# Moving a norm and a matrix difference in two slabs of a fused attention and MoE kernel, and storing the last slab with one DMA per 128-row block

## The chip, the cores and the metric

The kernel runs on one core of a Trainium2 chip. The metric is device time in microseconds (us); a profiled execution is taken apart instruction by instruction. The engines are TensorE (PE in the profile, its weight loads PEld), VectorE (DVE), ScalarE (ACT), GpSimd (POOL) and SyncE (SP), which here only issues DMAs and waits. Sixteen DMA engines move the data.

## The reference, cut to what matters

Attention with a softmax of its own on q and on k, eight batches of eight heads, 576 positions, head size 64; then a gated layer over all 4608 tokens of width 512 with 2048 hidden units:

```python
q_s = exp(q - max(q, -1));  q_s = q_s / (sum(q_s, -1) + 1e-9)     # over the head size
k_s = exp(k - max(k, 2));   k_s = k_s / (sum(k_s, 2) + 1e-9)      # over the positions
kv  = einsum('bhsd,bhse->bhde', k_s, v)
x   = einsum('bhsd,bhde->bhse', q_s, kv)   # -> (4608, 512), heads side by side
h   = x @ w_in;  g = h * sigmoid(beta * h);  out = g @ w_out
```

The kernel leaves the maxima out (the inputs are small) and works in bfloat16 between the stages.

## The kernel before, in words

**Slabs.** The tokens are cut into nine slabs of 512. Slab t below 8 holds the first 512 positions of batch t; slab 8 holds the last 64 positions of all eight batches. For every slab `pass1_tile` and `pass1_lead` multiply x by `w_in` (line 406) and ScalarE applies the gate into `GT` (L744), VectorE scaling it (L767). Then `pass2_fast` multiplies by `w_out` (L844). It uses a scheme with seven block products in place of eight: sums of gate halves (`g_sum1`, `g_sum2`), differences of gate halves (`g_diff`, L810, one VectorE instruction of 128x2048 elements each, in place in `GT`) and sums and differences of the weights.

**Pass 2 in order.** TensorE runs the products into three PSUM banks s, z5 and z2: s and the first part of z5, then z2 with `gs2(1)`, z5 with `gt(0, 0)`, z2 with `gt(NG, 1)`, z5 with `gt(0, 1)`, and z2 with `gt(NG, 0)`. The two products named last read what `g_diff(0)` and `g_diff(1)` have made: z5's last one the first, z2's last one the second. ScalarE empties z5 and z2 once each in between (`copy`, L880), and VectorE adds at the end (`last`, L892). z2's last product also needs ScalarE's copy out of z2, since it writes that bank again. `hooks` holds callbacks that are run at numbered places between those steps (`at(0)` to `at(7)`).

**Attention for the next batch** is woven into the slabs. `exp_q`, `exp_k` and `exp_kr` are ScalarE exponentials. `norm_main(b, hp0, n, eng, sums, mult)` normalises n head pairs of q: a VectorE sum (L357), a reciprocal (L359), and the multiply (L361), on VectorE or GpSimd. `turn` transposes the result with a DMA on SP's queue (L606), `norm_turn` is both with the multiply on GpSimd. Casts of v run on GpSimd (`casts`). `kv_steps` are the key-value products on TensorE (L482), after which VectorE writes a reciprocal and `KVD` (L490, L459). `quad(b, (g,))` (L554) multiplies the transposed q by `KVD`, half a batch at a time in slabs 1 to 3; the first half needs the first transpose DMA, the second half the second one. These steps are put in at counts of TensorE work: `todo` holds pairs of a count and a step, and `tick` runs the ones that are due. For slabs 1 and 2 `attn_late` puts the key-value products at 100 or 97 and the first half of `quad` at 118; the second half comes at 1.5 in the next slab.

**Order on each engine** is the order of recording: `add` appends an instruction to its engine's list, and `Program.plan` derives the semaphore waits from what is read and written. [...] A DMA's issue is one instruction of SP's or ScalarE's list, its end a semaphore of its own.

**Slabs 1 and 2 at place 3** run `diffs_norm`, one VectorE sequence:

```python
norm_main(b, 2, 2, mult=False)   # sum, reciprocal
g_diff(0); g_diff(1)
norm_main(b, 2, 2, sums=False)   # multiply, on VectorE
turn(b, 2, 2)
```

**The end.** Slabs 0 to 7 are stored by one DMA each on SP. Slab 8 is stored by `store8` as its parts get ready: `O2S[0]` holds four blocks of 128 rows, each made of 64 rows of two batches (the two partition halves), in two column halves. `emit` ends SP's list with a wait for each output semaphore, in the order of their names.

Of the kernel before, what the change touches and what calls it, by code (L numbers as in the profile page):

```python
# [7 lines left out]
ACT = mybir.ActivationFunctionType  # L8
# [5 lines left out]
S = 576  # L14
D = 64
NTOK = B * S
DM = H * D
# [6 lines left out]
SM = 512  # L24
# [5 lines left out]
PE, ACTE, DVE, POOL, SP = "tensor", "scalar", "vector", "gpsimd", "sync"  # L30
# [14 lines left out]
class Program:  # L45
# [12 lines left out]
    def add(self, eng, fn, r=(), w=(), bank=(), slot=None, after=(), war=False):  # L58
        op = Op(eng, fn, slot)
        op.pos = len(self.ops)  # L60
        deps = op.deps
        deps.extend(after)
        for k in r:
            deps.extend(self.writer.get(k, ()))
            self.readers.setdefault(k, []).append(op)
        for k in w:
            for d in self.readers.get(k, ()):
                if d is not op and (war or not self._same(d, op)):
                    deps.append(d)
            for d in self.writer.get(k, ()):  # L70
                if not self._same(d, op):
                    deps.append(d)
            self.readers[k] = []
            self.writer[k] = [op]
        for k in bank:
            t = self.touch.setdefault(k, {})
            for e, d in t.items():
                if e != eng:
                    deps.append(d)
            t[eng] = op  # L80
        if eng == POOL and slot is None:
            if self.pool is not None:
                deps.append(self.pool)
            self.pool = op
        self.ops.append(op)
        return op
# [42 lines left out]
    def emit(self, nc, es):  # L129
        counts, waits = self.plan()  # L130
        sems = {}
        for key in counts:
            sems[key] = es.enter_context(nc.semaphore("s_" + "_".join(str(x) for x in key)))
        by = {e: [] for e in (PE, ACTE, DVE, POOL, SP)}
        for op, w in zip(self.ops, waits):
            by[op.eng].append((op, w))

        def run(eng):
            def body(h):
                for op, w in by[eng]:  # L140
                    for key, n in w:
                        h.wait_ge(sems[key], n)
                    ins = op.fn(h)
                    if op.slot is not None:
                        ins.then_inc(sems[op.count[0]], 16)
                    elif op.inc:
                        ins.then_inc(sems[op.count[0]], 1)
                if eng == SP:
                    for key, n in sorted(counts.items(), key=str):
                        if key[0] == "dma" and str(key[1]).startswith("out"):  # L150
                            h.wait_ge(sems[key], n)
            return body

        with nc.Block() as blk:
            for e in (PE, ACTE, DVE, POOL, SP):
                getattr(blk, e)(run(e))


def bass_efficient_attn_shen__then__act_swish_beta_kernel(
# [10 lines left out]
    win_h, wout_h, beta_h, out_h = moe_w_in.tensor, moe_w_out.tensor, moe_beta.tensor, out.tensor  # L170

    with ExitStack() as es:
# [53 lines left out]
        add = P.add  # L226
# [122 lines left out]
        def norm_main(b, hp0, n, eng=DVE, sums=True, mult=True):  # L349
            i = b % 2  # L350
            a = bass.AP(EQ[i], hp0 * 512, [[2048, 128], [64, 8 * n], [1, 64]])
            s_ = bass.AP(QS[i], hp0 * 8, [[32, 128], [1, 8 * n]])
            v_ = bass.AP(QI[i], hp0 * 8, [[32, 128], [1, 8 * n]])
            vb = bass.AP(QI[i], hp0 * 8, [[32, 128], [1, 8 * n], [0, 64]])
            ks = [("eq", i, hp) for hp in range(hp0, hp0 + n)]
            if sums:
                add(DVE, lambda e: e.tensor_reduce(s_, a, AX.X, ALU.add), r=ks,  # L357
                    w=[("qs", i, hp0)])
                add(DVE, lambda e: e.reciprocal(v_, s_), r=[("qs", i, hp0)], w=[("qi", i, hp0)])  # L359
            if mult:  # L360
                add(eng, lambda e: e.tensor_tensor(a, a, vb, ALU.mult), r=ks + [("qi", i, hp0)],  # L361
                    w=ks)
# [239 lines left out]
        def turn(b, hp0, n):  # L602
            i = b % 2
            o = bass.AP(QT[i], hp0 * 512, [[2048, 128], [128, 4 * n], [1, 128]])
            a = bass.AP(EQ[i], hp0 * 512, [[2048, 128], [1, 512 * n]])
            add(SP, lambda e: e.dma_start_transpose(o, a),  # L606
                r=[("eq", i, hp) for hp in range(hp0, hp0 + n)],
                w=[("qt", i, hp) for hp in range(hp0, hp0 + n)], slot=f"tq{i}{hp0}")
# [14 lines left out]
        def one(fn, *a):  # L623
            return lambda: fn(*a)

        def steps(fn, *a):
            return lambda: go(fn(*a))
# [7 lines left out]

        def attn_late(b):
            if b < 4:
                return [(100 if b == 2 else 97, steps(kv_all, b)), (118, one(quad, b, (0,)))]
            return [(96, steps(kv_all, b)), (99, lambda: g_diff(1)), (112, one(quad, b))]

        def spread(steps, lo, hi):
# [135 lines left out]
            add(SP, lambda e: e.dma_start(a, O2S[t % 2][:, :, :]),  # L777
                r=[("o2", t % 2, u, d) for u in range(4) for d in range(2)], slot=f"out{t % 2}")

        def store8(th, dh, u=None):  # L780
            us = (0, 1) if u is None else (u,)
            n = len(us)
            for h in range(2):
                a = bass.AP(out_h, ((4 * th + h + 2 * us[0]) * S + SM) * DM + 256 * dh,
                            [[DM, 64], [2 * S * DM, n], [1, 256]])
                o = O2S[0][64 * h:64 * h + 64, 2 * th + us[0]:2 * th + us[0] + n,
                           256 * dh:256 * dh + 256]
                add(SP if h == 0 else ACTE, lambda e, o=o, a=a: e.dma_start(a, o),
                    r=[("o2", 0, 2 * th + u_, dh) for u_ in us], slot=f"outr{th}{dh}{h}{us[0]}")

        def gv(f, th, n):
            return GT[:, f:f + n, 256 * th:256 * th + 256]
# [15 lines left out]
        def g_diff(fh):  # L808
            f, th = NG * fh, 1 - fh
            add(DVE, lambda e: e.tensor_tensor(gv(f, th, NG), gv(f, th, NG), gv(f, 1 - th, NG),  # L810
                                               ALU.subtract),
                r=gk(f, 0, NG) + gk(f, 1, NG), w=gk(f, th, NG), war=True)
# [20 lines left out]
        def pass2_fast(t, tick, hooks):  # L833
# [53 lines left out]
            def last(bk, th, dh):  # L887
                o, w = out(th, dh)
                ts = TS[:, :].rearrange("p (a b) -> p a b", b=256)
                h = halves(bk)  # L890
                for b_, u0, u1 in h:
                    add(DVE, lambda e, b_=b_, u0=u0, u1=u1: e.tensor_tensor(  # L892
                        o[:, u0:u1, :], ts[:, u0:u1, :], bank3(b_)[:, u0:u1, :], ALU.add),
                        r=["ts", ("ps", b_)], w=w[u0:u1], bank=[b_])
                    if t == 8 and len(h) == 2:
                        store8(th, dh, u0)
                if t == 8 and len(h) == 1:
                    store8(th, dh)

# [53 lines left out]
        for t in range(NSLAB):  # L953
# [88 lines left out]
            def on(n, fn, *a):  # L1042
                hooks.setdefault(n, []).append(lambda: fn(*a))
# [4 lines left out]
                if b % 2 == 0:  # L1048
                    exp_kr(b)

            def diffs_norm(b):
                norm_main(b, 2, 2, mult=False)
                g_diff(0)
                g_diff(1)
                norm_main(b, 2, 2, sums=False)
                turn(b, 2, 2)

            def casts(b):
                g = P.writer[("gs2", NG - 1)]
# [5 lines left out]
            if t == 1:  # L1065
                on(0, exps, 2)
                on(0, casts, 2)
                on(2, norm_turn, 2, 0)
                on(3, diffs_norm, 2)
                on(3, load, 4)  # L1070
            elif t == 2:
                on(0, exps, 3)
                on(2, norm_turn, 3, 0)
                on(3, diffs_norm, 3)
                on(3, load, 5)
                on(4, exp_q, 4)
                on(4, casts, 4)
                on(6, norm_turn, 4, 0)
            elif t == 3:
                on(0, exp_k, 4)  # L1080
                on(0, exp_kr, 4)
                on(0, exp_q, 5)
                on(3, g_diff, 0)
                on(4, norm_turn, 5, 0)
                on(5, norm_turn, 5, 2)
                on(4, exp_qr, 1)
                on(5, exp_k, 5)
                on(5, norm_turn_rem)
                on(5, casts, 5)
                on(5, load, 6)  # L1090
                on(7, load_rem, "qrf", qt_h, QRF, 4)
            elif t + 2 < B:
                b = t + 2
                on(0, exps, b)
                on(0, casts, b)
                if t == 4:
                    on(0, load, 7)
                on(3, norm_turn, b, 0)
                on(4, norm_turn, b, 2)
# [40 lines left out]
```

## Time and profile before

| | |
|---|---|
| median of three runs | 274.03 us (273.77 to 274.29) |
| the profiled execution's own time | 274.5 us |
| its span, first to last instruction | 272.4 us |
| TensorE busy | 262.3 us (96%) |
| VectorE, ScalarE, GpSimd busy | 193.9, 180.8, 58.8 us |
| TensorE idle ahead of `quad` in slab 1, in slab 2 | 0.97, 1.55 us |
| slab 8's stores, on SP and on ScalarE | 3 of 128 KB and 2 of 64 KB on each |
| from issue to landing, 128 KB (SP, ScalarE) | 2.6, 2.9 us |
| from issue to landing, 64 KB (SP, ScalarE) | 2.4, 2.6 us |

The span is what the instructions and waits of the core take; the measured time has some 2 us around it. Busy shares are averages over stages, so what a change is worth has to be read from the waits at its place. A line of the time line gives the start and the length in us, the engine, the source line, the operation, what is written and read, how many instructions are merged into it, and in brackets how long the engine was idle before and what it waited for.

### The profile page before, as it was taken

The numbers are of one execution on the slowest core, as the hardware profiler recorded it, in microseconds if no ns is written. First come the engines' busy times: TensorE is split into PE (matmuls) and PEld (weight loads), VectorE is DVE, ScalarE is ACT, GpSimd is POOL, SyncE is SP. The second block draws the span as 40 slices with busy tenths as digits, with TensorE's granted clock in tenths as the row PEclk, the third lists the DMA queues.
The fourth block names the chain that finished last, engine by engine and source line by source line (L and its number), as shares of the span: only waits on it lengthen the run. The fifth ranks groups of instructions, "written<-read, shape, count | busy, mean of one in ns | idle before, by whom it ended". The sixth has DMA issues, their size and how long they took to land.

```text
span 272.4 us, 4985 instructions
## 1 busy us (share of the span) xinstructions
PE 262.3 (96%) x1974; PEld 163.5 (60%) x1993; DVE 193.9 (71%) x409; ACT 180.8 (66%) x287; POOL 58.8 (22%) x78
## 2 busy tenths in 40 slices
PE   8999999999899989999999999999999999999994
PEld 2444454448744864468645874587458745874683
DVE  4964586887958798868778885888488549625762
ACT  4898568789277955887778938893783387018610
POOL 2790010006130086100820651036000100000000
PEclk9999999999999999999999999999999999999999
DMA  7999999989799228960399899603600130012005
GB/s 219 318 201 207 227 326 350 288 236 370 157 328 285 82 42 231 293 211 2 63 261 298 252 359 162 193 1 79 213 2 0 22 154 0 2 58 99 0 2 155
DMA packets 59367, 45.95 MB, mean 169 GB/s; under 512 B 28608, under 2 KB 58320, under 8 KB 58320
## 3 DMA queue, kind: packets, MB, share of 16 engines
q1 hardware_dynamic: 54480, 40.90, 53.8%
q0 software_dynamic: 4240, 4.19, 9.3%
q10 hardware_dynamic: 624, 0.53, 0.6%
q8 instruction: 16, 0.26, 0.4%
q14 instruction: 7, 0.06, 0.1%
HBM read 36.71 MB, written 9.44 MB: 169 GB/s over the span
## 4 chain that ended last, share of the span: by engine, by line
PE 81%; DVE 12%; DMA 2%; SPq 2%; issue 1%; ACT 0%; DVEq 0%
PE PS L406 48%; PE PS L844 30%; DVE QS L357 3%; DMA VF<-in_v_dram 2%; DVE GT L810 2%; DVE EQ L361 2%; PE PS L554 1%; PE PS L482 1%; SPq L278 1%; SPq L290 1%; DVE QI L359 1%; DVE O2S L892 1%; DVE VB L377 1%; DVE TS L913 1%; DVE TS L916 1%
## 5 line engine op out<-in xcount | busy, mean ns | idle before, releaser
L406 PE MATMUL PS<-XT,WIN 128*128 128x512 bf16 x560 | 125.4, 379 | 1.5 <-issue 0.3
L744 ACT ACTIVATE GT<-PS,BETA 128x512 bf16<-128x512 f32 x144 | 95.0, 689 | 37.4 <-PE PS L406 37.2
L406 PEld LDWEIGHTS PS<-XT,WIN 128*128 128x128 bf16 x576 | 55.0, 98 | 65.2 <-DVE XT L596 1.1
L767 DVE TENSOR_SCALAR GT<-GT,RB 128x512 bf16<-128x512 bf16 x144 | 52.5, 386 | 38.4 <-ACT GT L744 37.7
L844 PE MATMUL PS<-WOUT,GS 128*128 128x256 bf16 x256 | 31.1, 273 | 0.0
L361 POOL TENSOR_TENSOR EQ<-EQ,QI 128x1024 bf16<-128x1024 bf16 (+1 forms) x11 | 20.0, 1822 | 50.5 <-DVE QI L359 50.2
L844 PE MATMUL PS<-WOUT,GT 128*128 128x256 bf16 x256 | 29.8, 273 | 0.0
L844 PE MATMUL PS<-WSUM,GT 128*128 128x256 bf16 x256 | 29.8, 273 | 0.0
L880 ACT COPY O2S<-PS 128x512 f32<-128x512 f32 (+1 forms) x17 | 9.4, 560 | 27.6 <-PE PS L844 27.6
L844 PEld LDWEIGHTS PS<-WSUM,GT 128*128 128x128 bf16 x256 | 24.8, 98 | 3.7 <-issue 0.9
L844 PEld LDWEIGHTS PS<-WOUT,GT 128*128 128x128 bf16 x256 | 24.8, 98 | 2.9
L844 PEld LDWEIGHTS PS<-WOUT,GS 128*128 128x128 bf16 x256 | 24.8, 98 | 3.0
L319 ACT ACTIVATE EQ<-QF 128x512 bf16<-128x512 f32 x32 | 17.9, 619 | 7.5 <-DMA QF<-in_q_dram 7.4
L803 DVE TENSOR_TENSOR GS<-GT 128x512 bf16<-128x512 bf16 (+2 forms) x32 | 21.9, 685 | 0.0
L377 POOL CAST VB<-VF 128x512 bf16<-128x512 f32 x24 | 16.4, 682 | 25.4 <-DVE GS L803 13.2
L810 DVE TENSOR_TENSOR GT<-GT 128x2048 bf16<-128x2048 bf16 x16 | 20.3, 1301 | 0.0
L357 DVE TENSOR_REDUCE QS<-EQ 128x16 f32<-128x1024 bf16 (+1 forms) x20 | 19.7, 985 | 0.7 <-ACT EQ L319 0.7
L319 ACT ACTIVATE EK<-KF 128x512 bf16<-128x512 f32 x32 | 18.1, 620 | 0.2 <-DMA KF<-in_k_dram 0.2
L892 DVE TENSOR_TENSOR O2S<-TS,PS 128x512 f32<-128x512 f32 (+1 forms) x17 | 10.7, 644 | 9.3 <-PE PS L844 9.3
L844 PE MATMUL PS<-WSUM,GS 128*128 128x256 bf16 x128 | 16.6, 273 | 0.0
L406 PE MATMUL PS<-WOUT,GT 128*128 128x512 bf16 x62 | 15.0, 379 | 0.1
L844 PEld LDWEIGHTS PS<-WSUM,GS 128*128 128x128 bf16 x128 | 12.5, 98 | 3.2
(88 smaller groups left out, 211.2 us busy)
## 6 DMA issues: line engine op xcount, KB each, us to landing
out_dram<-O2S SPq DMA_DIRECT2D x8, 1024.0 KB, 5.0
QF<-in_q_dram SPq DMA_DIRECT2D x6, 1024.0 KB, 6.7
KF<-in_k_dram SPq DMA_DIRECT2D x6, 1024.0 KB, 9.3
VF<-in_v_dram SPq DMA_DIRECT2D x6, 1024.0 KB, 12.5
KF<-in_k_dram SPq DMA_DIRECT2D x8, 256.0 KB, 5.5
VF<-in_v_dram SPq DMA_DIRECT2D x8, 256.0 KB, 5.5
WOUT<-in_moe_w_out_dram POOLq DMA_DIRECT2D x4, 512.0 KB, 16.4
WIN<-in_moe_w_in_dram POOLq DMA_DIRECT2D x3, 512.0 KB, 9.1
```

Of the source, the lines that this page charges most:

```text
L319: add(ACTE, lambda e, o=o, a=a: e.activation(o, a, ACT.Exp), r=[(name + "f", i, hp)], w=[("e" + name, i, hp)])
L357: add(DVE, lambda e: e.tensor_reduce(s_, a, AX.X, ALU.add), r=ks, w=[("qs", i, hp0)])
L361: add(eng, lambda e: e.tensor_tensor(a, a, vb, ALU.mult), r=ks + [("qi", i, hp0)], w=ks)
L377: add(eng, lambda e: (e.copy if eng == ACTE else e.tensor_copy)(o, a), r=[("vf", i, hp), ("vone", i)], w=[("vb", i, hp)], after=after)
L406: add(PE, lambda e: e.matmul(o, l, r_, start=start, stop=stop), r=r, w=w, bank=[bk])
L744: add(ACTE, lambda e: e.activation(GT[:, f, :], PS[bk][:, :], ACT.Silu, scale=BETA[:, f:f + 1]), r=[("ps", bk), "beta"], w=[("gt", f, 0), ...
L767: add(DVE, lambda e: e.tensor_scalar(GT[:, f, :], GT[:, f, :], RB[:, f:f + 1], None, ALU.mult), r=k + ["rb"], w=k)
L803: add(DVE, lambda e: e.tensor_tensor(GS2[:, i:i + n, :], GT[:, i:i + n, :], GT[:, i + NG:i + NG + n, :], ALU.add), r=[k_ for f in (i, i + ...
L810: add(DVE, lambda e: e.tensor_tensor(gv(f, th, NG), gv(f, th, NG), gv(f, 1 - th, NG), ALU.subtract), r=gk(f, 0, NG) + gk(f, 1, NG), w=gk(f ...
L844: add(PE, lambda e, l=l, r_=r_, st=st, u=u, i=i, b_=b_: e.matmul(PS[b_][:, 256 * u:256 * u + 256], l, r_, start=st, stop=end and i == NG - ...
L880: add(eng, lambda e, b_=b_, u0=u0, u1=u1: (e.copy if eng == ACTE else e.tensor_copy)(o[:, u0:u1, :], bank3(b_)[:, u0:u1, :]), r=[("ps", b_ ...
L892: add(DVE, lambda e, b_=b_, u0=u0, u1=u1: e.tensor_tensor(o[:, u0:u1, :], ts[:, u0:u1, :], bank3(b_)[:, u0:u1, :], ALU.add), r=["ts", ("ps ...
```

## The change

It has three parts.

First, `diffs_norm` is gone. In slabs 1 and 2 place 3 now runs `norm_turn` for the second half of q, so that its multiply is on GpSimd too, and then `g_diff(0)` alone. `g_diff(1)` moves into `attn_late`, a tenth of a count after the key-value products, so that on VectorE it stands behind the reciprocals and `KVD` instead of ahead of them.

Second, place 4 of slabs 1 and 2 gets a small activation with the gate function, `silu_table`. ScalarE's switch of function tables, which the compiler puts ahead of the first instruction that needs another set, so moves from the slab's end to between the copies out of z5 and z2. In slab 2 it comes after the four exponentials of `exp_q(4)`, which stay at that place.

Third, slab 8's stores: eight DMAs in place of ten, one for each block of 128 rows and 256 columns, all issued by SP. The pattern of the DMA's DRAM side is now two batches of 64 rows of 1 KB, against 128 partitions. The waits at the end follow the order of issue.

```diff
+        last = {op.count[0]: op.pos for op in self.ops if op.slot is not None}
...
-                    for key, n in sorted(counts.items(), key=str):
-                        if key[0] == "dma" and str(key[1]).startswith("out"):
-                            h.wait_ge(sems[key], n)
+                    for key in sorted((k for k in counts if str(k[1]).startswith("out")),
+                                      key=lambda k: last[k]):
+                        h.wait_ge(sems[key], counts[key])
...
         def attn_late(b):
             if b < 4:
-                return [(100 if b == 2 else 97, steps(kv_all, b)), (118, one(quad, b, (0,)))]
+                x = 100 if b == 2 else 97
+                return [(x, steps(kv_all, b)), (x + .1, lambda: g_diff(1)),
+                        (118, one(quad, b, (0,)))]
...
-        def store8(th, dh, u=None):
-            us = (0, 1) if u is None else (u,)
-            n = len(us)
-            for h in range(2):
-                a = bass.AP(out_h, ((4 * th + h + 2 * us[0]) * S + SM) * DM + 256 * dh,
-                            [[DM, 64], [2 * S * DM, n], [1, 256]])
-                o = O2S[0][64 * h:64 * h + 64, 2 * th + us[0]:2 * th + us[0] + n,
-                           256 * dh:256 * dh + 256]
-                add(SP if h == 0 else ACTE, lambda e, o=o, a=a: e.dma_start(a, o),
-                    r=[("o2", 0, 2 * th + u_, dh) for u_ in us], slot=f"outr{th}{dh}{h}{us[0]}")
+        def store8(th, dh, us=(0, 1)):
+            for u in us:
+                a = bass.AP(out_h, ((4 * th + 2 * u) * S + SM) * DM + 256 * dh,
+                            [[S * DM, 2], [DM, 64], [1, 256]])
+                o = O2S[0][:, 2 * th + u, 256 * dh:256 * dh + 256]
+                add(SP, lambda e, o=o, a=a: e.dma_start(a, o),
+                    r=[("o2", 0, 2 * th + u, dh)], slot=f"outr{th}{dh}{u}")
...
-                        store8(th, dh, u0)
+                        store8(th, dh, (u0,))
...
-            def diffs_norm(b):
-                norm_main(b, 2, 2, mult=False)
-                g_diff(0)
-                g_diff(1)
-                norm_main(b, 2, 2, sums=False)
-                turn(b, 2, 2)
+            def silu_table():
+                add(ACTE, lambda e: e.activation(DUMMY[:, 2:3], WARM[:, 0:1], ACT.Silu),
+                    r=["warm"], w=["dummy"])
...
-                on(3, diffs_norm, 2)
+                on(3, norm_turn, 2, 2)
+                on(3, g_diff, 0)
+                on(4, silu_table)
...
-                on(3, diffs_norm, 3)
+                on(3, norm_turn, 3, 2)
+                on(3, g_diff, 0)
                 on(3, load, 5)
                 on(4, exp_q, 4)
+                on(4, silu_table)
```

## The prediction

> **What bounds the kernel now.** I read the page first: shares of busy time, then the DMA queues.
>
> ```profile
> span 272.4 us, 4985 instructions
> PE 262.3 (96%) x1974; PEld 163.5 (60%) x1993; DVE 193.9 (71%) x409; ACT 180.8 (66%) x287; POOL 58.8 (22%) x78
> ...
> q1 hardware_dynamic: 54480, 40.90, 53.8%
> ...
> q10 hardware_dynamic: 624, 0.53, 0.6%
> ```
>
> TensorE is busy for 262.3 of 272.4 us, so a change to the slabs can only win the few gaps. Queue q1 is SP's, q10 ScalarE's. Next the time line of TensorE in slabs 1 and 2, at `quad`:
>
> ```profile
> 73.05 0.41 PE L554 MATMUL PS<-QT,KVD 64*64 64x512 bf16 x4 [0.97 <-DVE KVD L459]
> 73.40 2.03 PE L844 MATMUL PS<-WSUM,GT 128*128 128x256 bf16 x17
> ```
>
> ```profile
> 102.47 0.41 PE L554 MATMUL PS<-QT,KVD 64*64 64x512 bf16 x4 [1.55 <-DVE RC L490]
> ...
> 106.82 2.55 PE L406 MATMUL PS<-XT,WIN 128*128 128x512 bf16 x11 [0.23 <-DVE XT L596]
> ```
>
> Both gaps are put down to VectorE, whose key-value step stands behind two differences and a multiply. But `quad` has two waits, and the one in brackets need not be the last. The waits of the weight loads for slab 1 name the other:
>
> ```profile
> engine line waited for: us in total, times, longest us
> PEld PS L554 <- DMA QT<-EQ: 1.7, 2, 1.2
> ```
>
> In slab 1 TensorE passed VectorE's semaphore at 72.75 us, and the first transpose, issued at 68.92, landed at 73.01; the weight load began at 73.05. In slab 2 the transpose landed at 100.88 and VectorE was late (102.4). So only slab 2's gap is VectorE's. Last, the tail of the time line (SP, then VectorE's last sum):
>
> ```profile
> 264.15 5.51 SPq L788 DMA_DIRECT2D out_dram<-O2S  x5
> 264.16 0.73 ACTq L788 DMA_DIRECT2D out_dram<-O2S  x1
> 265.12 0.65 ACT L880 COPY O2S<-PS 128x256 f32<-128x256 f32 x2 [0.99 <-PE PS L844]
> 265.80 4.09 ACTq L788 DMA_DIRECT2D out_dram<-O2S  x4
> ...
> 268.72 0.42 DVE L892 TENSOR_TENSOR O2S<-TS,PS 128x256 f32<-128x256 f32 x1 [0.45 <-PE PS L844]
> ```
>
> After 269.14 nothing is left but the last stores (issued at 269.17 and 269.28, landed at 271.46 and 271.64) and SP's waits, to 272.36. Whatever delays a store here is paid in full.
>
> [...] every DMA before has a slowest dimension of 16, 64 or 128 on both sides and 16 landings. [...] at 108.61 a gate scaling that takes 0.34 us alone took 1.75, until GpSimd's multiply (108.32 to 110.22) was over.
>
> **Part 1, norms and keys.** VectorE loses a multiply (1.21 us) ahead of the keys, and a difference (1.2 us) moves behind them. GpSimd gains a multiply of 1.90 us per slab.
>
> Slab 1: `quad` still waits for the transpose of 73.01, whose multiply isn't touched. Gain 0. `g_diff(0)` runs 68.72 to 69.95; GpSimd's second multiply waits for it, then 69.95 to 71.85; the keys end at 70.8 (they read PSUM, and at 102.04 one took its usual 0.29 us beside a GpSimd cast); `g_diff(1)` waits for GpSimd until 71.85 and ends near 73.0. z2's last product, its only reader, comes at 73.5: cover of 0.5 us. Behind it on VectorE is the cast of x, which needs `quad` and comes at 73.5 anyway. The second transpose is issued at 71.85 instead of 72.28, ahead of batch 4's loads; nothing later waits.
>
> Slab 2: `g_diff(0)` 97.57 to 98.8, GpSimd's multiply then to 100.7, the keys to 99.6. `quad` starts when the transpose has landed, 100.92 instead of 102.47. `g_diff(1)` ends near 101.9. The v casts behind the moved multiply end near 105.7; their reader is a slab away. SP's second transpose goes at 100.7 (before 101.95), the loads behind it likewise.
>
> **Part 2, the table.** The switch costs 1.28 us and the small activation 0.2 (both rows are in the trace). In slab 1 ScalarE idles 2.02 us between its copies: hidden. In slab 2 it doesn't: exponentials to 100.38, switch to 101.66, activation to 101.87, copy out of z2 0.57, ready at 102.47. So z2's last product starts at 102.52 instead of 102.94: of 1.55 us, 0.42 is left, and a new wait for ScalarE takes the rest. Behind that copy on ScalarE is only a cast of x that TensorE needs at 105. Behind it VectorE's sums come earlier, and the 0.23 us gap at 106.82 (0.40 in starts) should close. Slab 2 gains 0.42 + 0.40 = 0.82 us; bounds 0.3 (gap stays, casts collide) and 1.6. Slabs 3 to 8 have no wait on a DMA in TensorE's chain and shift as a whole.
>
> **Part 3, the stores.** Each of the eight is 128 rows of 1 KB. Its DRAM pattern now has slowest size 2 (batches), its SBUF side 128. [...] The price of a piece: 1 MB loads put 64 such pieces on an engine, and two in a row landed at 80.51 and 83.53, 3.02 us apart, 47 ns a piece; ScalarE's queue, which carries 512 pieces, shows 0.6% of 16 x 272.4 = 26 us, 51 ns. So one store takes 3.0 us, eight 8 x 64 x 47 ns = 24.1 us (51 ns: 26.1; 45: 23.0). SP can issue one each 0.65 us, so the queue never runs dry: z5's first two are ready at 264.15, the next two at 265.8, four by 269.2.
>
> Sum on the profiled span: first issue 264.15 - 0.82 = 263.33; first piece 1.32 later (before, 265.47 after 264.15): 264.65; eight stores 24.1: 288.75; landing 0.4 after the last piece: 289.15. Then 0.5 to the end instead of 0.72, since the reordered list has one wait left after the last landing instead of five of 0.06 us: 289.65. That is 17.3 over 272.36. On the median, which lies 1.7 above that span: 274.03 + 17.3 = **291.3 us**.
>
> **Rivals.** *Sixteen engines after all* (0.12): [...] a store lands some 2.5 us after issue. SP's chain of four issues at the end costs 0 to 0.44 us, the landing up to 0.2, the waits give 0.24 back: about 0. Left is slab 2's gain: 274.03 - 0.8 = 273.2, faster. It decides if the last store lands within about 3.3 us of its issue. For it: the SBUF side has 128 rows. Against: the DRAM side has 2. *Two engines, but other ones each time* (0.03): only the last store counts, issued at 268.8 + 1.32 + 3.0 + 0.4 + 0.5 = 274.0, 1.7 over: 275.7. *The slabs lose* (0.01): [...] `quad` in slab 2 starts no earlier than before and z2 waits for `g_diff(1)`, up to 1.9 us each slab: with the slow stores 274.03 + 18.1 + 3.8 = 296. A like wait for the transpose alone, with no gain at all, ends at 292.1 and is in the likeliest's own range.
>
> **How the numbers follow.** Two engines, the same for all: 0.84, own range 289.0 (45 ns a piece and a gain of 1.6) to 294.5 (51 ns, no gain, one late landing). It holds 0.95 of that case, 0.80 in all, so it is the range. Faster needs sixteen engines and a gain over 0.55 us (0.2%, about what a measurement tells from no change): 0.09; within 0.2%: 0.03; slower 0.88.
>
> **What would show it.** Right: SP's stores land 3 us apart and the last one 20 us after its issue; DMA in the last slices at about two sixteenths; the span's chain ends in a DMA of some 20 us; TensorE's last product about 0.8 us earlier; in slab 1 `quad` still at 73.05 behind the transpose, in slab 2 at 100.92 and then a wait of about 1.1 us for ScalarE's copy. Wrong: stores landing 2.5 us after issue[...], landings far apart from 3 us (the price), a later `quad`[...].

## The result and the profile after

The changed kernel takes 289.02 us (median of 4 runs, 288.86 to 289.40), the kernel before beside it 274.16 us (4 runs, 273.77 to 274.31). The ratio is 1.054, with a 95% interval of 1.0527 to 1.0559: 14.9 us slower. The profiled execution took 288.86 us with a span of 287.1.

First the page of the kernel after: span and busy time by engine, the busy tenths of TensorE and of the DMA engines in 40 slices of 7.2 us, the two hardware queues, and the shares of the chain that ended last.

```profile
span 287.1 us, 4988 instructions
PE 262.7 (92%) x1974; PEld 163.7 (57%) x1993; DVE 192.7 (67%) x407; ACT 181.4 (63%) x289; POOL 63.9 (22%) x80
...
PE   8999999999999989999999999999999999999200
...
DMA  7999999997894299404989991171003002100111
...
q1 hardware_dynamic: 54928, 41.43, 50.8%
...
q10 hardware_dynamic: 32, 0.01, 0.0%
...
PE 85%; DVE 6%; ACT 2%; issue 1%; DVEq 0%
```

TensorE's work is the same (262.7 against 262.3 us), but its last three slices are nearly empty. In those slices the DMA row reads 1: the engines are a tenth to two tenths busy, while nothing else runs. The chain that ended last, on the page's last line here, contains no DMA at all and so doesn't explain the tail: it is followed back from the last computing instruction, which is VectorE's last sum, and leaves out what comes after it. Neither does the list of DMA issues explain it, whose last column should be the time to landing:

```profile
out_dram<-O2S SPq DMA_DIRECT2D x8, 128.0 KB
```

The column is missing for these eight stores. The trace's records have only two completion writes for each of them (packets of 4 bytes behind a store's data, each followed by an update of its semaphore), against sixteen for every store of slab 8 before, and in the runs here the profile gives slab 8's stores a landing where they have sixteen and none where they have two, four or eight. So the empty column is itself a sign to look for. The time line of the tail, SP's issues and VectorE's last sum, shows where the time is:

```profile
262.44 16.05 SPq L788 DMA_DIRECT2D out_dram<-O2S  x8
...
267.02 0.42 DVE L892 TENSOR_TENSOR O2S<-TS,PS 128x256 f32<-128x256 f32 x1 [0.45 <-PE PS L844]
```

The last sum ends at 267.44, and SP then still issues stores until 278.5. The windows view (length, busy time of each engine with its instructions, granted clock, share of the 16 DMA engines, GB/s) takes the stretch after it:

```profile
core 0: us, PE busy (x) PEld busy (x) DVE busy (x) ACT busy (x) POOL busy (x), PEclk, DMA share, GB/s
...
267.40:286.60 19.20, 0.00 (x0) 0.00 (x0) 0.04 (x1) 0.00 (x0) 0.00 (x0) 0.56 0.13 47
```

For 19.2 us no engine computes, and 0.13 of sixteen DMA engines are busy: about two engines, moving 47 GB/s. Put together from the trace's records, the eight stores are:

| store | issued | issue took | landed | after the one before |
|---|---|---|---|---|
| 1 | 262.44 | 0.7 | 267.59 | |
| 2 | 263.18 | 0.5 | 270.31 | 2.72 |
| 3 | 263.81 | 0.8 | 273.02 | 2.71 |
| 4 | 264.67 | 3.1 | 275.72 | 2.70 |
| 5 | 267.84 | 2.6 | 278.46 | 2.74 |
| 6 | 270.50 | 2.6 | 281.17 | 2.71 |
| 7 | 273.18 | 2.6 | 283.88 | 2.71 |
| 8 | 275.85 | 2.6 | 286.58 | 2.70 |

From the end of the last sum to the end of the span are 19.6 us, against 3.2 before (269.14 to 272.36): 16.4 lost. The slabs give 1.7 back (the first store is issued at 262.44 instead of 264.15). The difference is the 14.7 us by which the span grew.

The time line of the slabs (TensorE in slab 1, then TensorE, ScalarE, VectorE and GpSimd in slab 2) shows the gain:

```profile
71.75 0.41 PE L555 MATMUL PS<-QT,KVD 64*64 64x512 bf16 x4
72.10 0.28 PE L844 MATMUL PS<-WSUM,GT 128*128 128x256 bf16 x1
72.60 1.91 PE L844 MATMUL PS<-WSUM,GT 128*128 128x256 bf16 x16 [0.23 <-DVE GT L810]
...
100.00 0.41 PE L555 MATMUL PS<-QT,KVD 64*64 64x512 bf16 x4
100.34 0.28 PE L844 MATMUL PS<-WSUM,GT 128*128 128x256 bf16 x1
101.61 1.92 PE L844 MATMUL PS<-WSUM,GT 128*128 128x256 bf16 x16 [0.99 <-ACT O2S L880]
...
99.58 1.28 ACT L1052 ACT_TABLE_LOAD   x1
100.88 0.20 ACT L1052 ACTIVATE DUMMY<-WARM 128x1 f32<-128x1 bf16 x1
100.99 0.57 ACT L880 COPY O2S<-PS 128x512 f32<-128x512 f32 x1
...
96.65 1.26 DVE L810 TENSOR_TENSOR GT<-GT 128x2048 bf16<-128x2048 bf16 x1
...
98.64 2.12 DVE L810 TENSOR_TENSOR GT<-GT 128x2048 bf16<-128x2048 bf16 x1
...
94.93 4.74 POOL L362 TENSOR_TENSOR EQ<-EQ,QI 128x1024 bf16<-128x1024 bf16 x2 [13.90 <-DVE QI L360]
```

In both slabs `quad` (L555) now starts with no wait in brackets, 0.04 us after its transpose has landed (71.71 and 99.96). What waits instead is z2's last product: in slab 1 for `g_diff(1)`, in slab 2 for ScalarE's copy, which stands behind the switch of tables and the small activation. GpSimd's second multiply (96.91 to 99.67 by the trace's records) begins beside `g_diff(0)`, which ends at 97.91, and takes 2.76 us where the first one takes 1.90. `g_diff(1)`, begun beside the multiply at 98.64, takes 2.12 us where the one ahead of the keys takes 1.26, and ends 1.08 us after the multiply. The prediction counted on such waits. Its one example was an instruction of another form, a gate scaling with one tensor and a column of scalars (1.75 us instead of 0.34); that a difference of two tensors is slowed too was the author's estimate, and here it shows, with 0.86 us more for each of the two instructions.

### The profile page after: what moved, and what is told of

Same layout as the page of the kernel before. It is cut to its first block, busy times and chain, and to the rows that moved or that the text cites. A ratio compares the mean times of both kernels' runs of the same rounds, so it can differ in the third digit from the quotient of the medians.

```text
span 287.1 us, 4988 instructions
## 1 busy us (share of the span) xinstructions
PE 262.7 (92%) x1974; PEld 163.7 (57%) x1993; DVE 192.7 (67%) x407; ACT 181.4 (63%) x289; POOL 63.9 (22%) x80
## 4 chain that ended last, share of the span: by engine, by line
PE 85%; DVE 6%; ACT 2%; issue 1%; DVEq 0%
PE PS L407 51%; PE PS L844 31%; DVE QS L358 2%; PE PS L483 1%; PE PS L555 1%; DVE GT L810 1%; ACT EQ L320 1%; PE PS L405 1%; DVE EQ L362 0%; DVE QI L360 0%; ACT L1052 0%; ACT O2S L880 0%; DVE XT L512 0%; DVE TS L913 0%; DVE TS L916 0%
## 5 line engine op out<-in xcount | busy, mean ns | idle before, releaser
L362 POOL TENSOR_TENSOR EQ<-EQ,QI 128x1024 bf16<-128x1024 bf16 (+1 forms) x13 | 25.6, 1968 | 47.2 <-DVE QI L360 46.6
L810 DVE TENSOR_TENSOR GT<-GT 128x2048 bf16<-128x2048 bf16 x16 | 21.6, 1378 | 0.0
L798 DVE TENSOR_TENSOR GS<-GT 128x256 bf16<-128x256 bf16 (+2 forms) x32 | 13.6, 426 | 1.1
```

Of the source, the lines that this page charges most:

```text
L798: add(DVE, lambda e: e.tensor_tensor(GS1[:, i:i + n, :], gv(i, 0, n), gv(i + NG, 1, n), ALU.add), r=gk(i, 0, n) + gk(i + NG, 1, n), w=[("g ...
```

## The experiments

### The parts apart

The theory was that the stores lose all and the slabs gain a little. The first rival was that the slabs, or the waits in another order, share in the loss. One kernel is the kernel before with the new stores and the new order of the final waits alone (cut to the stores; the waits' edit is shown with the last kernel below):

```diff
+        def store8(th, dh, us=(0, 1)):
+            for u in us:
+                a = bass.AP(out_h, ((4 * th + 2 * u) * S + SM) * DM + 256 * dh,
+                            [[S * DM, 2], [DM, 64], [1, 256]])
+                o = O2S[0][:, 2 * th + u, 256 * dh:256 * dh + 256]
+                add(SP, lambda e, o=o, a=a: e.dma_start(a, o),
+                    r=[("o2", 0, 2 * th + u, dh)], slot=f"outr{th}{dh}{u}")
```

> The slabs as before, slab 8's stores and the order of the final waits as after. Theory A (each of the eight stores runs on two DMA engines, the same two for all): all of the slowdown is here, and the small gain of slabs 1 and 2 is gone: 290.2 us (289.8 to 290.8), eight landings 2.7 us apart, the last some 10.7 us after its issue. Rival B (the slabs themselves cost part of it): clearly under 289.

Measured: 290.46 us (290.15 to 291.79), ratio 1.060 (1.0576 to 1.0622), span 288.4. The stores land 2.71 us apart, the last at 287.87, and `quad` in slab 2 starts at 102.09: 0.38 us earlier than before, a lead that this execution already had at slab 1's `quad`. The other is the kernel before with the new slabs alone (cut to the order and to slab 2):

```diff
-                return [(100 if b == 2 else 97, steps(kv_all, b)), (118, one(quad, b, (0,)))]
+                x = 100 if b == 2 else 97
+                return [(x, steps(kv_all, b)), (x + .1, lambda: g_diff(1)),
+                        (118, one(quad, b, (0,)))]
...
-                on(3, diffs_norm, 3)
+                on(3, norm_turn, 3, 2)
+                on(3, g_diff, 0)
                 on(3, load, 5)
                 on(4, exp_q, 4)
+                on(4, silu_table)
```

> Slabs 1 and 2 as after, the stores and the final waits as before. Theory A: faster than before, by the 0.8 us forecast for slab 2, or by 1.3 if slab 1 gains 0.5 as the profile after suggests: 272.8 to 273.4 us. Rival B: slower than 274.16. In slab 1 the wait ahead of quad tells whether the transpose's landing at 73.01 before was that run's, or the place's: about 72.7 if it is the place's, about 71.7 if the run's.

Measured: 273.00 us (9 runs), ratio 0.996 (0.9942 to 0.9977), span 270.8. The two parts add up: the stores cost 290.46 - 274.21 = 16.2 us alone (with the new order of waits) and 289.02 - 273.00 = 16.0 on top of the slabs; the slabs gain 1.2 alone and 290.46 - 289.02 = 1.4 beside the stores.

### One queue, or the pattern

The new stores differ from the old in two ways: all go through SP, and the DRAM side has two batches outermost. The rival says that the single queue is the loss. The changed kernel with the old ten stores of 64 rows, all issued by SP:

```diff
-            for u in us:
-                a = bass.AP(out_h, ((4 * th + 2 * u) * S + SM) * DM + 256 * dh,
-                            [[S * DM, 2], [DM, 64], [1, 256]])
...
+            for h in range(2):
+                a = bass.AP(out_h, ((4 * th + h + 2 * us[0]) * S + SM) * DM + 256 * dh,
+                            [[DM, 64], [2 * S * DM, n], [1, 256]])
...
                 add(SP, lambda e, o=o, a=a: e.dma_start(a, o),
```

> After, with the ten stores of before (64 rows each side), but all ten issued by SP. Theory A: sixteen engines again, each store lands some 2.5 us after its issue; SP's row of ten issues costs at most 0.6 us at the end: 273.0 to 274.0 us. Rival C (it is one queue carrying all stores that is slow): 285 us or more.

Measured: 274.20 us (12 runs), ratio 1.000 (0.9992 to 1.001), span 272.6. So a single queue isn't the loss, though it costs a little more than expected: 1.2 us over the slabs alone. The list of DMA issues (count, KB each, median from issue to landing) has its last column again:

```profile
out_dram<-O2S SPq DMA_DIRECT2D x6, 128.0 KB, 2.4
...
out_dram<-O2S SPq DMA_DIRECT2D x4, 64.0 KB, 2.9
```

Most of the stores are as quick as before (the slowest took 4.0 us). What costs is that SP issues ten in a row, 0.65 us each and one 1.23, so the last is issued at 270.02 instead of 267.82. The opposite test keeps the new pattern and gives each pair to two queues:

```diff
-                add(SP, lambda e, o=o, a=a: e.dma_start(a, o),
+                add((SP, ACTE)[u], lambda e, o=o, a=a: e.dma_start(a, o),
```

> After, with the second block of each pair issued by ScalarE instead of SP, the DMAs themselves unchanged. Theory A: both queues feed the same two DMA engines, so 289 us again (288.5 to 289.5), the landings of the two queues interleaved 2.7 us apart. Rival C: half the work per queue, about 279 us.

Measured: 289.94 us (289.93 and 289.95), ratio 1.057 (1.055 to 1.0592). The time line shows both issuing engines held:

```profile
263.10 10.11 SPq L788 DMA_DIRECT2D out_dram<-O2S  x4
...
265.04 8.82 ACTq L788 DMA_DIRECT2D out_dram<-O2S  x3
```

The stores land in pairs, 270.84 and 271.60, 276.27 and 277.04, 281.71 and 282.46, 287.14 and 287.51: 5.43 us for two, the same 2.7 for one. So the two queues share the same two engines. The time is 0.4 us above the range expected, and the landings come in pairs instead of evenly spaced.

### The number of engines

If the outermost size of the DRAM side sets the number of engines, four batches give four engines and half the time, eight give eight. These two kernels change only the pattern in the kernel after; each store is still 128 pieces of 1 KB, but slab 8's rows land in other places of the output. Four batches:

```diff
-                a = bass.AP(out_h, ((4 * th + 2 * u) * S + SM) * DM + 256 * dh,
-                            [[S * DM, 2], [DM, 64], [1, 256]])
+                a = bass.AP(out_h, (4 * th * S + SM + 32 * u) * DM + 256 * dh,
+                            [[S * DM, 4], [DM, 32], [1, 256]])
```

Eight batches:

```diff
-                a = bass.AP(out_h, ((4 * th + 2 * u) * S + SM) * DM + 256 * dh,
-                            [[S * DM, 2], [DM, 64], [1, 256]])
+                a = bass.AP(out_h, (SM + 16 * (2 * th + u)) * DM + 256 * dh,
+                            [[S * DM, 8], [DM, 16], [1, 256]])
```

> After, each of the eight stores writing 32 rows of four batches instead of 64 rows of two; bytes, pieces of 1 KB, number of DMAs, queue and issue order unchanged, the rows of slab 8 come out permuted. Theory A (the DRAM side's slowest size sets the number of engines): four engines, 32 pieces each a store at 42.4 ns, 1.36 us a store, 10.9 us for eight against 21.7: 11 us less than after, 278 us (277 to 279.5). Rival D (the pattern of two batches is slow for another reason, such as rows far apart in DRAM): no better than 288.

> As the run with four batches, but 16 rows of eight batches a store. Theory A: eight engines, 0.68 us a store, 5.4 us for eight, about as fast as SP issues them: the end is now bound by the last issue, about 268, plus 2.5 us of landing and 0.5 to the end: 273.0 us (272.4 to 274). Rival D: no better than 288.

| outermost size | 1 KB pieces on an engine | completion writes a store | landings apart, us | last landing | time, us |
|---|---|---|---|---|---|
| 2 (after) | 64 | 2 | 2.71 | 286.58 | 289.02 |
| 4 | 32 | 4 | 1.60 and 1.45, then 1.35 to 1.41 | 276.61 | 279.1 (2 runs), ratio 1.017 (1.0131 to 1.0218) |
| 8 | 16 | 8 | 0.7 to 1.2 | 271.98 | 273.85 (10 runs), ratio 0.998 (0.9967 to 0.9994) |
| 64, ten stores on SP | 8 or 4 | 16 | 0.2 to 2.2 | 272.08 | 274.20 (12 runs), ratio 1.000 (0.9992 to 1.001) |

By the count of completion writes the stores ran on 2, 4 and 8 engines. From two to four the spacing of the landings halves. With eight, SP's own pace (an issue each 0.65 us) is nearly what remains: of the 16 us, 0.85 are left against the slabs alone (273.85 to 273.00). Rows far apart in DRAM (rival D) are not the cause, since the rows of one store lie in more batches here and the stores are faster. In these runs the number of engines was the outermost size of the DRAM side at 2, 4 and 8, and sixteen at 64; other sizes were not tried, and the SBUF side was 64 or 128 throughout.

### The slabs

In slab 2 the switch of tables stands ahead of a copy that z2 waits for. With the slabs alone, less the small activation there, the compiler's switch goes to the first gate activation:

```diff
                 on(4, exp_q, 4)
-                on(4, silu_table)
                 on(4, casts, 4)
```

> The slabs as after, but in slab 2 the small activation with the gate function is left out, so that the table is switched where it was before; stores and final waits as before. Theory A: z2's last product no longer waits for ScalarE's copy but for g_diff(1), 0.76 us earlier, and the switch at the slab's end costs at most 0.1: 272.2 us (271.9 to 272.6), against 273.0 with it. Rival E (the early switch is what wins in slab 2): 273.5 or more.

Measured: 272.48 us, ratio 0.994 (0.9916 to 0.996), span 270.4. ScalarE's time line:

```profile
99.75 0.57 ACT L882 COPY O2S<-PS 128x512 f32<-128x512 f32 x1
100.81 0.58 ACT L596 CAST XT<-PS 128x512 bf16<-128x512 f32 x1 [0.50 <-PE PS L554]
103.98 0.58 ACT L596 CAST XT<-PS 128x512 bf16<-128x512 f32 x1 [2.58 <-PE PS L554]
104.58 1.28 ACT L746 ACT_TABLE_LOAD   x1
105.91 0.69 ACT L746 ACTIVATE GT<-PS,BETA 128x512 bf16<-128x512 f32 x1
```

The copy ends at 100.3 instead of 101.8 (both against the slabs alone). The switch now fills the 1.17 us for which ScalarE, with the small activation, idles ahead of the first gate activation, and that activation still starts 0.02 us after TensorE has its tile ready (105.91, against 106.43). Before, the switch stood at the same place, and the gate activation behind it waited 0.26 us more for TensorE: there was nothing for the moved switch to win in slab 2. z2's last product starts at 101.17 instead of 101.86; its wait, by TensorE's time line, falls from 1.00 to 0.27 us and is then for `g_diff(1)`:

```profile
101.17 1.91 PE L846 MATMUL PS<-WSUM,GT 128*128 128x256 bf16 x16 [0.27 <-DVE GT L812]
```

Next, which half of the slab change gives the gain: the order on VectorE, or the multiply on GpSimd? In the kernel before with the order alone, the second multiply stays on VectorE, but moves behind the keys and `g_diff(1)` too (and the loads at place 3 to place 4, so that they stay behind its transpose):

```diff
+        def mult_turn(b):
+            norm_main(b, 2, 2, sums=False)
+            turn(b, 2, 2)
...
+                return [(x, steps(kv_all, b)), (x + .1, lambda: g_diff(1)),
+                        (x + .2, one(mult_turn, b)), (118, one(quad, b, (0,)))]
...
                 g_diff(0)
-                g_diff(1)
-                norm_main(b, 2, 2, sums=False)
-                turn(b, 2, 2)
```

> Before, with g_diff(1) behind the keys and the second multiply left on VectorE behind it, its transpose and the next loads after it on SP; tables, stores and waits as before. Theory A: quad's first half starts as early as after, but the second transpose leaves 1 to 1.5 us later than with GpSimd's multiply and the second half of quad waits for it by about that: the gain is mostly lost, 273.7 to 274.5 us. Rival F (the order alone brings the gain, GpSimd's multiply nothing): 273.0.

Measured: 276.62 us (8 runs, 275.28 to 278.63), ratio 1.008 (1.0049 to 1.0109), span 275.7. That is slower than before, and the expectation was wrong. TensorE's time line, at the second `quad` of slabs 1 and 2:

```profile
77.14 0.41 PE L554 MATMUL PS<-QT,KVD 64*64 64x512 bf16 x4 [1.76 <-DMA QT<-EQ]
...
107.22 0.41 PE L554 MATMUL PS<-QT,KVD 64*64 64x512 bf16 x4 [1.95 <-DMA QT<-EQ]
```

The multiply that I had let slip behind the keys feeds the second transpose. It is issued at 73.55 and 104.03 (after: 71.40 and 99.70), lands 3.1 to 3.6 us later, and the second `quad` waits for it. A further loss follows slab 2's stall. The windows view shows the granted clock (the last column but two) there:

```profile
104.00:108.40 4.40, 2.20 (x15) 0.85 (x14) 3.83 (x8) 0.62 (x2) 3.35 (x4) 1.00 0.62 137
108.40:112.00 3.60, 3.60 (x10) 1.36 (x10) 2.21 (x4) 2.81 (x4) 2.16 (x2) 0.53 1.08 367
112.00:116.00 4.00, 4.00 (x21) 1.81 (x19) 1.88 (x6) 3.09 (x6) 0.00 (x0) 1.00 1.11 350
```

Ahead of it TensorE was busy for half of 4.4 us; then it runs at 0.53 of its clock for about 3.5 us, eight matmuls 0.427 us apart instead of 0.216, some 1.6 us lost. The other half of the change, the multiply on GpSimd with both differences still ahead of the keys:

```diff
             def diffs_norm(b):
-                norm_main(b, 2, 2, mult=False)
+                norm_turn(b, 2)
                 g_diff(0)
                 g_diff(1)
-                norm_main(b, 2, 2, sums=False)
-                turn(b, 2, 2)
```

> Before, with the second multiply on GpSimd and nothing else: both differences stay ahead of the keys; tables, stores and waits as before. Theory A[...]: g_diff(1) waits for the multiply, the keys come no earlier than before, quad in slab 2 still waits 1.5 us or more: 274.0 to 274.8 us. Rival G (the multiply on GpSimd is what brings the gain): 273.0.

Measured: 274.52 us (12 runs), ratio 1.0015 (1.0001 to 1.0028): no gain. VectorE's time line in slab 2:

```profile
97.90 4.10 DVE L810 TENSOR_TENSOR GT<-GT 128x2048 bf16<-128x2048 bf16 x2
101.92 0.15 DVE L490 RECIPROCAL RC<-PS 128x2 f32<-128x2 f32 x1
```

In the kernel before the same stretch was:

```profile
97.57 2.80 DVE L810 TENSOR_TENSOR GT<-GT 128x2048 bf16<-128x2048 bf16 x2
100.29 1.63 DVE L361 TENSOR_TENSOR EQ<-EQ,QI 128x1024 bf16<-128x1024 bf16 x1
101.85 0.16 DVE L490 RECIPROCAL RC<-PS 128x2 f32<-128x2 f32 x1
```

The two differences, begun 0.33 us later, take 4.10 us beside GpSimd's multiply instead of 2.80, which uses up the 1.63 us of multiply that are no longer ahead of the keys, so the keys come no earlier, and `quad` still starts at 102.55. Neither of these two kernels gains. A third was not run: `g_diff(1)` behind the keys and the multiply left ahead of them on VectorE, so that the second transpose isn't delayed. So it isn't shown that the new order needs GpSimd's multiply.

Last, what the runs point to, in one kernel: the slabs without slab 2's small activation, the old stores on two queues, and only the final waits in the order of issue.

```diff
+        last = {op.count[0]: op.pos for op in self.ops if op.slot is not None}
...
-                    for key, n in sorted(counts.items(), key=str):
+                    for key in sorted((k for k in counts if str(k[1]).startswith("out")),
+                                      key=lambda k: last[k]):
```

> The slabs as after but without the small activation in slab 2, the stores of before, and the final waits in the order of issue as after. Theory A: as the same kernel with the waits in the order of names (272.5 us), less 0.2 us of waits behind the last landing: 272.3 us (271.9 to 272.6); from the last landing to the end of the span 0.5 us instead of 0.7. The best of the kernels run here.

Measured: 272.06 us (6 runs, 271.9 to 273.34), ratio 0.994 (0.9913 to 0.996), span 270.1. It is faster than both kernels. From the last landing (269.64) to the end are 0.49 us instead of 0.72. Against the same slabs without the new order of waits (272.48 us beside a before of 274.18) the ratio is the same within its interval, so what the waits give shows in the trace alone. TensorE in slab 2:

```profile
101.18 1.91 PE L847 MATMUL PS<-WSUM,GT 128*128 128x256 bf16 x16 [0.27 <-DVE GT L813]
```

## Why the prediction was right, and where it wasn't

The forecast, 291.3 us, was on the right side and for the right reason; the time measured, 289.02, lies 2.3 us below it and only 0.02 us inside the range, which is luck. The low end of 289.0 was to be 45 ns a piece and a gain of 1.6 us, but these two, put into the prediction's sum, give 289.5: without the half microsecond that the sum doesn't explain, the time would lie outside. Against the predicted span of 289.65 the profiled one is 2.6 us shorter:

| term | predicted | measured | difference |
|---|---|---|---|
| first store issued | 263.33 | 262.44 | -0.89 |
| to its first piece | 1.32 | 1.28 | -0.04 |
| all pieces of eight stores | 24.1 | 22.5 | -1.6 |
| last piece to landing | 0.4 | 0.33 | -0.07 |
| landing to end | 0.5 | 0.48 | -0.02 |

- **Two engines, the same for all: right.** That each store would put 64 of its 128 pieces on each of two engines was the author's estimate: no DMA of the kernel before had fewer than sixteen landings. Measured: landings evenly spaced (2.70 to 2.74 us), two completion writes a store, 0.13 of sixteen engines, and the spacing halved with four batches. The rival of sixteen engines and the one of other engines each time fall. Which two they are isn't shown: the records don't number the engines.
- **47 ns a piece: mis-sized, and so was the low bound of 45.** In the steady run a store took 2.717 us, 42.4 ns a piece; the first took 3.50, so 3.50 + 7 x 2.717 = 22.5 us. The price came from loads that ran on sixteen engines at once. With four engines the later stores took 1.35 to 1.41 us for 32 pieces, 42 to 44 ns each, so from two engines to four the price hardly rose. Whether a store's piece is cheaper than a load's, or few engines than sixteen, was not tried.
- **"SP can issue one each 0.65 us, so the queue never runs dry": the second half right, the first wrong.** After three stores an issue takes 2.6 us or more, and each of these issues ends within 0.21 us after the landing of the store three before it, as if SP were held until that one is done. So the last store lands 10.7 us after its issue and not 20. It cost nothing here, because the two engines always had work, but whatever stood behind these issues on SP would have been late.
- **Slab 2: right.** z2's last product gained 0.41 us and the gap at the later `XT` closed, another 0.38: 0.79 us measured against 0.82. The new wait for ScalarE was forecast as 1.1 us; it is 0.99 in brackets. `quad` started at 100.00 and not 100.92, which is the 0.92 us by which slab 1 had moved everything that follows.
- **Slab 1, "gain 0": the step that failed.** It took the transpose's landing of 73.01 as fixed. In this execution it landed at 71.71, 3.15 us after its issue instead of 4.08 (in the kernel with the new slabs alone at 71.96). `quad` then moved up to 71.75, which VectorE's earlier keys allowed, and z2's last product, now the one to wait, started at 72.60 instead of 73.52. Of these 0.92 us, 0.36 was there before slab 1's keys, where the two kernels do the same, and is that execution's; 0.55 is the gain (0.55 in the kernel with the new slabs alone too). Part of it needs no edit: with the old slabs and the new stores, slab 1 was 0.24 us shorter than in the profiled execution of the kernel before, merely since the transpose landed sooner. So the slabs are worth 1.2 to 1.4 us and not 0.8. In the kernel with the old slabs and the new stores, VectorE's semaphore came at 72.60 and the transpose landed at 72.63: the two were late almost together, and reading one execution's last wait as the only one was the mistake. When the landing is late is open: in all twelve traces it follows max(issue + 3.15, landing of slab 0's store on the same queue + 0.9) within 0.06 us, but no run moved that store.
- **The marks.** Evenly spaced landings, the share of two sixteenths and the new wait for ScalarE showed as said. "The span's chain ends in a DMA" did not: the chain is followed back from the last computing instruction, so it leaves the tail out whatever the stores do; in the kernel before, too, it ends with VectorE's last sum, 3.2 us before the end of the span. Beside the two completion writes the trace has one more update of each store's semaphore, 0.4 us after its issue has ended and 4.1 to 8.0 us before its landing; the stores before have none. What it is for, no run shows.
- **The switch of tables, forecast as hidden in slab 1 and paid in slab 2: right,** and worth more than the forecast let see: leaving it out of slab 2 brought a further 0.5 us (273.00 to 272.48, with ratios whose intervals overlap; by the traces 0.7 us at z2's last product and 0.5 in the span).

## What to carry to other kernels

Look at the outermost size of the DRAM side of a DMA's pattern before merging two DMAs into one: a 128-partition store whose DRAM side begins with two batches ran on two of sixteen engines (2.71 us a store), and a second queue did not make that good (289.94 us against 289.02). An empty landing column, a DMA share of 0.13, near two sixteenths, and two completion writes a store in the records were how the profile showed it; the chain that ended last left out the stores' tail in both kernels. When one wait is removed, list all that the instruction waits for and how far apart they come, over more than one execution; and ask of every step that is moved what waits for it and what it will run beside: the multiply, put behind the keys, delayed the second transpose (issued at 73.55 instead of 71.40 in slab 1); put on GpSimd with both differences still ahead of the keys, it slowed them (4.10 us instead of 2.80) by about as much as it freed (1.63 us, less a start 0.33 us later).

## What the hardware showed that was not expected

- The issuing engines were held while the stores ran on two DMA engines: from the fourth store on, SP's issue took 2.6 to 3.1 us instead of 0.5 to 0.8, and with two queues SP and ScalarE were held for up to 5.1 us at one issue. With four engines the longest issue was 1.04 us.
- After slab 2's stall in the kernel with the order alone, TensorE was granted about half its clock: 0.53 over 3.6 us, once it had been busy for half of the 4.4 us ahead (idle for 1.95 us at one time, 2.2 in all). What sets it off isn't shown. By the mean clocks it wasn't in every execution: of eight runs, four had a mean clock of 0.992 to 0.994 and spans of 274.6 to 276.5 us, four of 0.999 to 1.000 and 273.1 to 274.4.
- The first of the slow stores took 3.50 us from first to last piece, each later one 2.72. No run tells why.
